# One pool of seven PSUM banks, a last attention round in two halves, and a new order of issue

## The chip, the cores and the metric

The kernel runs on one NeuronCore of a Trainium2 chip. The metric is the device time of one execution in microseconds. In the tables PE is TensorE's matmul, PEld its weight load, DVE is VectorE, ACT is ScalarE, POOL is GpSimd and SP is SyncE, which issues most of the transfers.

## What is computed

For one sequence of 2048 tokens of width 448 the kernel computes two branches of the same input and mixes them with a gate for each token:

```
g = sigmoid((x * gate_w).sum(-1))
q, k, v = split(x @ wqkv)             # 16 heads of 28
p = softmax(q @ k.T * 28**-0.5)       # per head, 2048 x 2048
a = concat_heads(p @ v) @ wo
b = irfft2(rfft2(x) * (w_r + 1j*w_i)) # over tokens and width
out = g * a + (1 - g) * b
```

The softmax has 16 x 2048 x 2048 exponentials, the largest part of the work.

## The kernel before

**Attention.** The 16 heads form four groups of four; a head takes a strip of 32 partitions. The 2048 queries are cut into four chunks of 512. A pair (group, chunk) is a round, `n` = 0 to 15 in `groups`; round 15 is the last chunk of the last group. A round runs over 16 key blocks of 128 keys, and a *unit* is one head of one key block: a score matmul of 128 keys by 512 queries (32 rows of the array, "row" layout, one of four row strips), which fills one PSUM bank of 512 float32 columns.

A unit's exponential is made in one of two ways. `ND` gives, for each round, how many key blocks go the second way.

- *ScalarE* (kind "a"): two units at a time are scored into `psA` or `psB` (two banks each, taken in turn), and one ACTIVATE (L1034) of 1024 columns writes them to the ring (`ring`, 28 slots) in bfloat16. There are 374 of these steps.
- *VectorE* (kind "d"): a unit is scored into one of three banks `bg`; a TENSOR_SCALAR (L993, "eviction") turns the score into the bits of a bfloat16 number, and GpSimd adds three constants to these bits (INT64_ADD, L1003). That gives four phases of an approximate exponential, which are averaged through the value matmuls.

The value matmuls (`pv`) are done in "column" layout, four heads side by side in four column strips of 32. Four such matmuls, one for each head, are called a quad here. A key block on ScalarE needs one quad, a key block on VectorE four, one for each phase. All quads of a round accumulate in the bank `pvb`. A column of ones in the weights gives the softmax sums.

**Normalising.** When a round is done, `normalise` copies `pvb` to SBUF (L1166), brings the sums through DRAM to the layout in which they can be inverted and multiplied (L1169, L1178), all hidden behind the next round. The last round has no round behind it: it copies all 512 queries (L1137), forms the sums by small float32 matmuls, inverts them (L1146), broadcasts them by matmuls and multiplies in two pieces of 256 (L1159). Then `last_tile` projects the last four blocks of 128 tokens (k = 0 to 3 are the spectral branch, k = 4 to 7 the four head groups; k = 7 of these waits for the normalised last round), evicts them with the gate on VectorE (L1250) or ScalarE (L1246) and stores them. The other twelve blocks of tokens go through `out_tile` (L1224).

**Background.** Projections of q, k and v, the gate and the whole spectral branch (two-dimensional transform by matmuls, `fwd`, `mid`, `inv`) run between the attention work, through the same three banks `bg`. `Item` is the right to a bank for such a piece; `bgi` gives the bank.

**Order.** Every operation is registered with `Sched.op`, and nothing is emitted until `Sched.run`. That function reads `TABLE`, two packed lists found offline: the first is the order in which all 3639 operations are emitted (with six groups of filler matmuls that write zeros into `pvb`), the second the bank of each `Item`. `pin` keeps the emitted order on every engine, and each engine's queue works strictly in that order: an operation that waits holds up all behind it on the same engine. The semaphores between engines are set by the tile framework from the tiles that instructions read and write; `psA`, `psB`, `pvb` and the three `bg` are tiles of their own. All matmuls are recorded at L432, transposes at L435.

Of the kernel before, what the change touches and what calls it, by code (L numbers as in the profile page):

```python
# [36 lines left out]
DUE_P = 4.0  # L37
TABLE = (
    "eNoN1mNjWEsUQNHxnMG5SW2ltm3bNtPUtm3btm3bto3UdvveX9hf1jakJbHEkXCCJDqJQWKSWCQ2iUPikngkPiEkAUlIEpHEJAkJI0lJMpKc"
    "UJKCZCApSU6SiniSmuQijHQlQAKiCScZSRoiSXaSlkQlitQk6Ugmkp7UILVINZKNZCG5SVUSheQhWUkOUodkJiVJKRKNlCa1SV5SloSQUFKO"  # L40
    "1Cf5SH5SgBQiBUkxUp6UIRVJYVKEFCXFySZSgWwmlUgJ0oq0JVvIVrKStCPbyHayiqwmVcgOsoZMJGtJZTKJTCZTyFSyjqwnG0g3YpVXG8l0"
    "MoPMJLOIU7PJHDKX7CTziCDzySy/gCwkcWk8Gp8uIovJDL+ELCUJaEK6jKDaRRLRnqQxWU5WkECFqMQ0Ck1Co9JoNDqNQcNoTBqLxqZx6G6y"
    "h+wl+0ioak6iqqfkGXlOXpCXJILcIQ3IfhJJ7pID5B55RV6TKOo+eUMekI7kIXlEHpNo6iCJrqaRGKouOUSS0mQ0pupEYqnkNAU9TJ6Qt2SD"
    "j63ekfckjvpA4qp4qhc5Qo6SlDS+akGOkan0I/lEptHPpAlJoBKq6fQLSaS+Qip6nCRWJ0hqmkR9gxk0TH0lp8hpkoau8WnpGXKWJFX1SG9y"
    "jpwnF8hMepEkU61JOnqJXCZXyFVyjSRX18kNcpOkULfIbZKeplRlaAaakZ4kmWhinoSnUj+hLE2t0qhYvByNzcvTXxCNz/XpVFpVgX6H6Dy9"
    "oqYiHUQyqIzqG0nGm5HvJAaPyX+Qn6Qp+UUyqT+QWf2DSjSLyqo6k+okDk/OK9OGpArtSDvRuDwhX+ezqc60C82uEvD1PhEP439IUp5D/SX/"
    "CKGUMrrac9qV5lSCSqqoprkU0Kw0G81Oc9DcKif9TXLR3NRQS/PQPCovzUdTcEfzKk/z05keaUDj83wqhBagmWlBWogWpkVofpWFhtJ4vCgt"
    "RtuTNqQ47U4LqIw8E+9BS9Ke1PJCyhhtHC+oCqv0vIjiJgMvTaUppoqqtLy4siYlr0p70RKqGi2pqtNSKh0vrVJzYXrTUlSZYaSMKkHT8Bq0"
    "Jk3FmSmrsvFyipi/UF5l5dn5SFpB5eGjaEU1mlZSeXkOPobWopVVB/IbqqiqKhcfS535AdVUTg6mNq2ucvMaqh7tQurTBjQfr0NrKm9qqc+u"
    "MC/DG9J4Bk1dWlsV4XVUDNOI1FUFeEJTkNdTCUwjmpnXV1l4WV6IJzHFeQlegefnFXkDFcs0VDFNXFOTN1KNVWNandfg8U0TVZQnMk1VMhOY"  # L50
    "YryZim1K8lo8jglXIaa5qsRb08o8mklpWqgIVY6X5m1oW9qOtlItVXnenjbjrVUqE86/uaimB2mjEpsmtK1KbkJNO1WVN6XNeQQPM9X4F9de"
    "NeFNeQeV0Xx3P9xP98t1VN1oJ1WX1+MZTDjtoprT7qSz+u0iaBTzx1XhLWhX1ZK2591UJlOKd1cduPQ9lPLpTHrTU/VSrWhtXoeDN9763iqN"
# [69 lines left out]
def unpack(table):  # L122
    raw = [zlib.decompress(base64.b64decode(t)) for t in table]
    return np.frombuffer(raw[0], np.uint16).tolist(), np.frombuffer(raw[1], np.uint8).tolist()
# [1346 lines left out]
```

## Time and profile before

| | |
|---|---|
| runs | 380.36, 381.06, 381.08 us; median 381.06 |
| profiled execution | span 379.2 us from the first to the last instruction; its own time isn't given apart, the median is 1.9 us longer |
| granted TensorE clock | 1.000 over the span |
| busy share | PE 98%, ACT 93%, DVE 89%, POOL 62% |
| exponentials on ScalarE | 374, mean 1079 ns each |
| evictions on VectorE | 276, mean 681 ns each |
| additions on GpSimd | 207, mean 1038 ns each |

A row of a timeline gives start, duration, engine, line, operation, the tile written and read, shape and count, and in brackets the idle time before it with what ended it. Matmuls are pipelined, so a duration of 0.38 us holds the way through the array, and the distance of two starts is what a matmul costs. In the same way an ACTIVATE starts before the one ahead of it has ended. A window's row gives its length and then the busy time (and number of instructions) of PE, PEld, DVE, ACT and POOL, the granted clock, the share of the DMA engines and GB/s.

### The profile page before, as it was taken

The page shows a single profiled execution, that of the slowest core. Times are in us where ns is not written, and L with a number is a line of the kernel's source. Part 1 is how long each engine was busy: PE and PEld are TensorE (multiplying, and loading weights), DVE is VectorE, ACT ScalarE, POOL GpSimd, SP SyncE. Part 2 cuts the span into 40 slices and gives each one's busy share as a digit, 9 for nine tenths or more (in the row PEclk, how much of TensorE's full clock was granted, in tenths as well). Part 3 has the DMA queues.
Part 4 walks back from the last instruction along what each step waited for, and adds up shares of the span by engine and source line. Part 5 has one row for each costly group of instructions (what it writes and reads, how often), then busy time and mean ns, then how long its engine had stood idle before and what let it go on. Part 6 is the DMA issues. An engine that isn't in the chain of part 4 may idle for free.

```text
span 379.2 us, 12643 instructions
## 1 busy us (share of the span) xinstructions
PE 371.3 (98%) x5117; PEld 142.4 (38%) x5117; DVE 339.1 (89%) x665; ACT 351.1 (93%) x389; POOL 234.4 (62%) x264
## 2 busy tenths in 40 slices
PE   8999999999999999999999999999999999999996
PEld 6634223342433333234333434233333323433564
DVE  1768899999999999999999999999999999988744
ACT  2799999999999999999999999999999999999841
POOL 4446465866778866565553565778597778483510
PEclk9999999999999999999999999999999999999999
DMA  6511101010210112211322212223222122222132
GB/s 145 157 34 44 29 18 36 4 36 2 41 52 22 44 41 54 55 38 30 68 60 93 69 40 49 57 61 70 45 64 74 30 69 72 86 64 72 35 103 75
DMA packets 31158, 21.23 MB, mean 56 GB/s; under 512 B 16260, under 2 KB 29052, under 8 KB 31100
## 3 DMA queue, kind: packets, MB, share of 16 engines
q1 hardware_dynamic: 29708, 19.96, 20.7%
q8 instruction: 40, 0.66, 0.7%
q10 hardware_dynamic: 1392, 0.46, 0.5%
q14 instruction: 18, 0.15, 0.1%
HBM read 14.51 MB, written 1.96 MB: 43 GB/s over the span
## 4 chain that ended last, share of the span: by engine, by line
PE 55%; ACT 31%; issue 6%; DVE 4%; DMA 2%; POOL 1%; SPq 0%; DVEq 0%; ACTq 0%; POOLq 0%
ACT ring L1034 31%; PE bg L432 24%; PE pvb L432 17%; PE psA L432 7%; PE psB L432 6%; DVE pd L993 2%; PE bg L435 1%; DMA CS<-cCS 1%; DVE X L1419 1%; POOL pd L1003 1%; DMA Wg<-in_B_w_i_dram 0%; DVE X L1298 0%; DVE q L1178 0%; DVE t L1362 0%; DVE wpq L1224 0%
## 5 line engine op out<-in xcount | busy, mean ns | idle before, releaser
L1003 POOL INT64_ADD pd<-pd x207 | 211.9, 1038 | 96.7 <-DVE pd L993 27.4
L1034 ACT ACTIVATE ring<-psA 128x1024 bf16<-128x1024 f32 x187 | 201.7, 1078 | 4.7 <-PE psA L432 3.2
L1034 ACT ACTIVATE ring<-psB 128x1024 bf16<-128x1024 f32 x187 | 201.7, 1079 | 2.6 <-PE psA L432 1.4
L993 DVE TENSOR_SCALAR pd<-bg 128x512 uint16<-128x512 f32 x276 | 180.9, 681 | 8.5 <-PE bg L432 3.5
L432 PE MATMUL pvb<-pd,vd 128*32 128x512 bf16 x1104 | 96.9, 384 | 0.1
L432 PE MATMUL bg<-q,k 32*128 32x512 bf16 x276 | 96.3, 383 | 0.2
L432 PEld LDWEIGHTS <-k 32*128 32x128 bf16 x1024 | 40.1, 91 | 122.4 <-issue 117.7
L432 PE MATMUL psB<-q,k 32*128 32x512 bf16 x374 | 73.2, 383 | 1.3 <-ACT ring L1034 0.7
L432 PE MATMUL psA<-q,k 32*128 32x512 bf16 x374 | 72.8, 383 | 0.5 <-ACT ring L1034 0.2
L432 PE MATMUL pvb<-ring,vw 128*32 128x512 bf16 x748 | 67.9, 384 | 0.0
L432 PEld LDWEIGHTS <-vd 128*32 128x32 bf16 x1104 | 25.3, 94 | 35.5 <-issue 31.1
L432 PEld LDWEIGHTS <-vw 128*32 128x32 bf16 x748 | 17.5, 94 | 22.7 <-issue 20.5
L432 PEld LDWEIGHTS <-xT 128*128 128x128 bf16 (+5 forms) x512 | 20.3, 97 | 10.7 <-issue 9.7
L432 PE MATMUL bg<-xT,wpq 128*32 128x512 bf16 (+3 forms) x244 | 21.2, 383 | 0.1
L1362 DVE TENSOR_TENSOR t<-bg,Wg 128x450 bf16<-128x450 f32 x32 | 18.8, 614 | 0.6 <-DMA Wg<-in_B_w_i_dram 0.4
L432 PE MATMUL bg<-xT,wpk 128*32 128x512 bf16 (+2 forms) x240 | 18.9, 383 | 0.0
L432 PE MATMUL bg<-wvr,xT 128*128 128x112 bf16 (+2 forms) x192 | 13.7, 213 | 0.0
L1178 DVE TENSOR_TENSOR q<-pvs,Rb 128x512 bf16<-128x512 f32 x15 | 10.9, 729 | 2.6 <-DMA Rb<-rsc 2.6
L1298 DVE TENSOR_TENSOR X<-bg,oc 128x226 bf16<-128x226 f32 (+1 forms) x32 | 12.3, 386 | 0.5
L432 PEld LDWEIGHTS <-CS 128*32 128x32 bf16 x384 | 9.0, 95 | 9.9 <-issue 5.6
L432 PE MATMUL bg<-xtok,CS 128*32 128x225 bf16 (+1 forms) x192 | 11.2, 294 | 0.7 <-DMA CS<-cCS 0.7
L742 DVE TENSOR_SCALAR k<-bg 128x512 bf16<-128x512 f32 x15 | 10.3, 685 | 1.3 <-PE bg L432 1.1
(117 smaller groups left out, 315.4 us busy)
## 6 DMA issues: line engine op xcount, KB each, us to landing
Rb<-rsc SPq DMA_DIRECT2D x60, 64.0 KB
CS<-cCS SPq DMA_DIRECT2D x16, 192.0 KB
V<-xtok SPq DMA_DIRECT2D x16, 113.0 KB
Wg<-in_B_w_i_dram SPq DMA_DIRECT2D x64, 28.1 KB
xtok<-Ab SPq DMA_DIRECT2D x16, 112.5 KB
xtok<-in_A_x_dram SPq DMA_DIRECT2D x3, 448.0 KB
Wg<-in_B_w_r_dram SPq DMA_DIRECT2D x32, 28.1 KB
out_dram<-wpq SPq DMA_DIRECT2D x6, 112.0 KB
```

The source lines that it names most:

```text
L432: self.pin(self.nc.tensor.matmul(out, lhsT=lhsT, rhs=rhs, start=start, stop=stop, **kw))
L435: self.pin(self.nc.tensor.transpose(out=out, in_=in_, identity=self.c("ident")[0:n, 0:n]))
L742: self.pin(nc.vector.tensor_scalar(out=dst, in0=self.bgi(it), scalar1=SQ, scalar2=None, op0=ALU.mult))
L993: self.pin(nc.vector.tensor_scalar(out=ys[:, s, :].bitcast(U16), in0=self.bgi(it), scalar1=127 * UNITS, scalar2=0.0, op0=ALU.add, op1=ALU. ...
L1003: self.pin(nc.gpsimd.int64_add(out=fl(pds), in0=fl(ys), in1=PHASE[f] * 0x0001000100010001))
L1034: self.pin(nc.scalar.activation(out=self.ring[:, u0:u0 + len(st), :], in_=slot[:, 0:len(st), :], func=ACT.Exp, scale=LN2 / UNITS))
L1178: e = self.dve(dv(512), lambda: self.pin(nc.vector.tensor_tensor(out=dst, in0=pvs[:], in1=self.Rb[:], op=ALU.mult)), ds, kk, lk=True)
L1298: self.pin(nc.vector.tensor_tensor(out=free_dims(self.X1[:, t, :], [[F, 2], [-1 if dif else 1, n]], (F - 1) * dif), in0=free_dims(self.bgi ...
L1362: self.pin(nc.vector.tensor_tensor(out=out[:], in0=self.bgi(it)[:, 0:F2].rearrange("p (a f) -> p a f", a=2), in1=free_dims(Wg[:], [[F, 2], ...
L1419: self.pin(nc.vector.tensor_tensor(out=free_dims(self.zt[0:FN], [[128, 4], [1, 128]], 512 * t), in0=self.bgi(it)[0:FN, :].rearrange("p (a ...
```

## The change

- **Banks.** `psA`, `psB` and the three `bg` become one tile `ps` of seven banks; `pvb` stays. Every score unit, the first transposes and the first projections get an `Item` and thereby any of the seven banks. A step of ScalarE reads two adjacent banks, whichever they are. An eviction on VectorE may take two adjacent banks in one instruction; `PARTS` lists how the four units of a key block can be grouped.
- **Dependencies.** Since all banks are in one tile, `pin` declares instructions that touch different banks independent, except where the operation names the other as needed (`need`) or both are on one engine.
- **Last round.** `ND` of round 15 goes from 3 to 1. Its queries are split into two halves of 256. A unit of this round covers two key blocks for one half, so that it still fills a bank (`HALF`, `tiles`, `score_mm`). Half 0 comes first, with seven ScalarE units per head and the one VectorE block; its values accumulate in a bank of the pool, those of half 1 in `pvb`. `normalise_half` normalises each half by itself.
- **Order.** `TABLE` is new and holds four lists: order (3972 operations, no fillers), banks, the number of units of each ScalarE step (378 times 2), and the grouping of the evictions of each of the 67 VectorE blocks (41 with four single ones, 24 with one pair, 2 with two pairs). A score is one operation for each unit now. `tstart` and the due times worked out from it are gone, which only served the planning.

The diff, cut to its core:

```diff
-    ND = [2,4,5,5]+[5,5,4,4]+[4,4,5,5]+[5,5,4,3]
+    ND = [2, 4, 5, 5, 5, 5, 4, 4, 4, 4, 5, 5, 5, 5, 4, 1]
...
-        self.psA = ps.tile([P, 2, 512], F32, name="psA")
-        self.psB = ps.tile([P, 2, 512], F32, name="psB")
+        self.ps = ps.tile([P, 7, 512], F32, name="ps")
         self.pv = ps.tile([P, 512], F32, name="pvb")
-        self.bgt = [ps.tile([P, 512], F32, name=f"bg{i}") for i in range(3)]
...
     def pin(self, ins):
...
+        if self.sc.used:
+            used = frozenset(self.sc.used)
+            keep = [p for p, u in self.sc.need() if not used & u]
+            if ins.ins.engine in self.before:
+                keep.append(self.before[ins.ins.engine])
+            for other in self.bank_sets:
+                if not used & other:
+                    self.tc.declare_no_dep(ins.ins, group="bank" + repr(sorted(other)), reason="other banks",
+                                           keep=[k for k in keep if k.name in self.bank_sets[other]])
...
+    HALF = [(0, i) for i in range(6)] + [(1, i) for i in range(6)] + [(1, 6), (1, 7), (0, 6), (0, 7)]
+
+    def tiles(self, n, v):
+        if n < 15:
+            return [(v, 0)]
+        kp = self.HALF[v][1]
+        return [(2 * kp, 0), (2 * kp + 1, 256)]
...
+    def score_mm(self, n, v, s, it):
+        g, c = self.groups[n]
+        w = 256 if n == 15 else 512
+        q0 = 512 * c + 256 * self.half(n, v)
+        for kt, o in self.tiles(n, v):
+            self.mm(self.bgi(it)[:, o:o + w], self.k[g][32 * s:32 * s + 32, 128 * kt:128 * kt + 128],
+                    self.q[g][32 * s:32 * s + 32, q0:q0 + w], True, True, tile_position=(32 * s, 0))
...
+                    self.pin(nc.vector.tensor_scalar(
+                        out=free_dims(ys[:], [[512 * e, w], [1, 512]], 512 * part[0]).bitcast(U16),
+                        in0=self.ps[:, bs[0]:bs[0] + w, :],
+                        scalar1=127 * UNITS, scalar2=0.0, op0=ALU.add, op1=ALU.max))
...
+                self.pin(nc.scalar.activation(out=self.ring[:, u0:u0 + len(st), :],
+                                              in_=self.ps[:, bs[0]:bs[0] + len(st), :],
+                                              func=ACT.Exp, scale=LN2 / UNITS))
...
+    def normalise_half(self, h, last, it):
...
+        o = 256 * h
+        ev = self.dve(0.42, lambda: self.pin(nc.vector.tensor_copy(out=pvs[:, o:o + 256], in_=bank()[:, 0:256])),
+                      last + [self.nlast[1]], -100.0)
...
+        def fsum():
+            for j in range(2):
+                self.mm(bank()[:, 256 + 4 * j:260 + 4 * j], pvs[:, o + P * j:o + P * j + P], rows, True, True)
+        m = self.pe(1024, fsum, [ev, self.d_cst2], kk, dur=0.45)
+        b = self.dve(0.2, lambda: self.pin(nc.vector.reciprocal(out=rr[:, 8 * h:8 * h + 8], in_=bank()[:, 256:264])),
+                     (m, self.nlast[1]), kk)
...
+        mb = self.pe(1024, fb, [b, self.d_idf], kk, mode="col", dur=0.45)
+        e = self.dve(0.42, lambda: self.pin(nc.vector.tensor_tensor(out=dst, in0=pvs[:, o:o + 256], in1=bank()[:, 0:256],
+                                                                    op=ALU.mult)), (mb,), kk, free=it)
+        self.onormt[12 + 2 * h] = self.onormt[13 + 2 * h] = e
```

455 lines of the change are left out of this document (243 added, 212 removed).

## The prediction

> **What bounds the kernel now.** I read the page first, then ScalarE's own rows in order of time, the busy time by windows, the groups kept apart by shape, and last the timeline of TensorE around one switch of work and around the end.
>
> ```profile
> PE 371.3 (98%) x5117; PEld 142.4 (38%) x5117; DVE 339.1 (89%) x665; ACT 351.1 (93%) x389; POOL 234.4 (62%) x264
> PE 55%; ACT 31%; issue 6%; DVE 4%; DMA 2%; POOL 1%; SPq 0%; DVEq 0%; ACTq 0%; POOLq 0%
> ```
>
> Three engines are nearly full, and the chain that ended last runs mostly through PE, a third through ScalarE. The rows of ScalarE say which of them gives the pace, and where.
>
> ```profile
> L1034 ACT ACTIVATE ring<-psA 128x1024 bf16<-128x1024 f32 x187 | 201.7, 1078 | 4.7 <-PE psA L432 3.2 <-PE psB L432 1.3 <-ACT ring L1034 0.2
> L1034 ACT ACTIVATE ring<-psB 128x1024 bf16<-128x1024 f32 x187 | 201.7, 1079 | 2.6 <-PE psA L432 1.4 <-PE psB L432 1.2
> ...
> 12.74 1.02 ACT L1034 ACTIVATE ring<-psA 128x1024 bf16<-128x1024 f32 x1 [0.31 <-PE psB L432]
> ...
> 17.32 1.02 ACT L1034 ACTIVATE ring<-psA 128x1024 bf16<-128x1024 f32 x1
> ...
> 20.03 1.06 ACT L1034 ACTIVATE ring<-psB 128x1024 bf16<-128x1024 f32 x1
> ...
> 156.00 1.02 ACT L1034 ACTIVATE ring<-psA 128x1024 bf16<-128x1024 f32 x1 [0.16 <-ACT ring L1034]
> ...
> 199.61 1.02 ACT L1034 ACTIVATE ring<-psA 128x1024 bf16<-128x1024 f32 x1 [0.46 <-PE psB L432]
> ...
> 341.94 1.05 ACT L1034 ACTIVATE ring<-psA 128x1024 bf16<-128x1024 f32 x1
> ...
> 364.96 1.02 ACT L1034 ACTIVATE ring<-psB 128x1024 bf16<-128x1024 f32 x1
> ```
>
> One exponential lasts 1.02, but the next starts before it ends: from 17.32 to 20.03 three steps take 2.71, so 0.903 us a step when nothing is missing. There are 374, hence 373 steps, 336.8 us. From the first at 12.74 to the last at 364.96 pass 352.2, so ScalarE loses 15.4 us between them. The rows numbered 154, 198 and 352 say where: 44 steps from 156.00 to 199.61 (39.7 due, 43.6 taken) lose 3.9, 21 steps from 341.94 to the end lose 4.1, and the other 308 steps lose 7.4. The windows agree:
>
> ```profile
> 160.00:200.00 40.00, 40.00 (x584) 14.99 (x588) 38.95 (x77) 37.52 (x42) 22.09 (x23) 1.00 0.20 48
> 200.00:340.00 140.00, 137.74 (x1789) 49.07 (x1785) 135.65 (x277) 139.69 (x153) 97.76 (x99) 1.00 0.25 62
> 340.00:366.00 26.00, 26.00 (x482) 11.89 (x486) 17.39 (x28) 22.84 (x25) 10.63 (x11) 1.00 0.26 75
> 366.00:379.20 13.20, 9.67 (x244) 7.02 (x236) 6.80 (x12) 1.55 (x2) 0.00 (x0) 0.99 0.22 72
> 40.00:340.00 300.00, 296.91 (x3993) 104.15 (x3996) 290.09 (x577) 297.01 (x325) 204.07 (x208) 1.00 0.19 48
> ```
>
> Where ScalarE (fourth busy figure) falls back, 37.52 of 40 and 22.84 of 26, PE is busy without a gap. So the time is: 12.7 until the first exponential, 336.8 of steps, 15.4 lost in them, and 14.2 from the start of the last one to 379.2. The median of the runs, 381.06, lies 1.9 us above this span; I add that to every span below.
>
> **What the edits cost, by part.** *More exponentials.* The last round gives two key blocks, eight units of 512 columns, back to ScalarE. Its 378 steps of two units (the list of widths in the new table holds 378 twos) are four more: +3.6 us at 0.903. Nothing hides them.
>
> *TensorE.* Prices first.
>
> ```profile
> 346.12 0.39 PE L432 MATMUL psB<-q,k 32*128 32x512 bf16 x2
> 346.44 0.39 PE L432 MATMUL bg<-wpk,q 128*32 128x448 bf16 x4
> ...
> 347.30 0.40 PE L432 MATMUL pvb<-ring,vw 128*32 128x512 bf16 x4
> 347.52 0.39 PE L432 MATMUL pvb<-pd,vd 128*32 128x512 bf16 x4
> 347.85 0.39 PE L432 MATMUL bg<-q,k 32*128 32x512 bf16 x1
> 347.85 0.39 PE L432 MATMUL psB<-q,k 32*128 32x512 bf16 x2
> 347.86 0.38 PE L432 MATMUL bg<-q,k 32*128 32x512 bf16 x1
> 348.17 0.40 PE L432 MATMUL pvb<-ring,vw 128*32 128x512 bf16 x4
> ```
>
> Four value matmuls side by side follow the next four after 0.22 (347.30 to 347.52). From values to scores it is 0.33 (347.52 to 347.85), from scores to the next group 0.32: each change between the row layout of the scores and the column layout costs 0.10 more. And two scores (346.12) or four in four strips (347.85) cost the same 0.32. So a run of scores costs 0.2 for entering and leaving and 0.217 for each set of different strips. Unpacked, the old order has 357 such runs with 381 sets, the new one 317 with 360: 40 x 0.2 + 21 x 0.217 = 12.6 us less. A key block on VectorE takes four phases of values, one on ScalarE a single one: two blocks moved save 2 x 3 quads, 1.3 us. Six filler groups go, 0.6. By these prices the whole order falls from 351.7 to 337.2 us. In the last round each score becomes two matmuls of 256 columns; whether the second set of weights is hidden no row shows in the row layout, so 0 (as for 224 columns in column layout below) to 64 x 0.09 / 3 = 1.9 us; I take 0.
>
> ```profile
> 353.33 0.56 PE L432 MATMUL bg<-Bd,X 113*32 113x224 bf16 x16
> ...
> L432 PEld LDWEIGHTS <-k 32*128 32x128 bf16 x1024 | 40.1, 91 | 122.4 <-issue 117.7
> ```
>
> Four such quads take 0.56, the last itself 0.27: 0.10 a quad, no weights seen.
>
> *VectorE and GpSimd.*
>
> ```profile
> 347.67 2.48 DVE L993 TENSOR_SCALAR pd<-bg 128x512 uint16<-128x512 f32 x4
> ...
> L993 DVE TENSOR_SCALAR pd<-bg 128x512 uint16<-128x512 f32 x276 | 180.9, 681 | 8.5 <-PE bg L432 3.5 <-PE psB L432 1.2 <-PE psA L432 0.9
> L1315 DVE CAST Ab<-bg 128x450 bf16<-128x450 f32 x16 | 9.8, 618 | 0.1
> ```
>
> Four evictions in 2.48, the last 0.68 long, are 0.60 apart. A column costs (681 - 618) / 62 = 1.02 ns, so 512 columns 0.52 and an instruction 0.08 (bounds 0 and 0.16, the fixed part of the 681). The parts list merges 28 pairs and eight evictions are gone, 240 instead of 276: 8 x 0.60 + 28 x 0.08 = 7 us less. GpSimd loses six additions; it is 62% busy. Neither shortens the chain by itself.
>
> *What this does to the lost 15.4.* I cut both orders into stretches of 22 exponentials (19.9 us of ScalarE) and price the work listed in each. After the start, PE stands clearly above 19.9 in three of the old: 154 to 198 with 21.4 and 21.7 (3.3 over; 3.9 were lost) and 352 to 374 with 22.2. That is where the rows lose time, so I trust the count. After, 154 to 198 comes to 39.0, below; new heavy ones are 198 to 220 (PE 21.4, VectorE 21.7), VectorE at 132 (20.9) and 308 (20.5), and the end (PE 21.4). Lost after: 154 to 198 0.7; 198 to 220 1.8 + 0.3; 132 1.0 + 0.2; 308 0.6 + 0.3; the end 4.1 - 0.8 = 3.3. The other steps lost 5.1 before. In the old order a step is mostly listed with only its own two units scored (312 of 374); with seven common banks the new one has four or six ready at 210 of 378, so a late score is covered by 0.9 us or more. I take 3.0 (bounds 1.7 and 5.1). Sum 11.2, a gain of 4.2.
>
> *The end.*
>
> ```profile
> 366.55 0.69 DVE L1137 COPY pvs<-pvb 128x512 f32<-128x512 f32 x1 [0.17 <-PE pvb L432]
> 367.80 1.05 PE L432 MATMUL pvb<-cst,pvs 128*128 128x4 f32 x8
> 368.89 0.26 DVE L1146 RECIPROCAL rr<-pvb 128x16 f32<-128x16 f32 x1 [0.40 <-PE pvb L432]
> ...
> 369.46 0.61 PE L432 MATMUL pvb<-sq,rr 128*32 128x128 f32 x16
> 370.15 0.42 DVE L1159 TENSOR_TENSOR q<-pvs,pvb 128x256 bf16<-128x256 f32 x1 [1.00 <-PE pvb L432]
> ...
> 371.40 0.62 PE L432 MATMUL pvb<-sq,rr 128*32 128x128 f32 x16
> 372.33 0.40 DVE L1159 TENSOR_TENSOR q<-pvs,pvb 128x256 bf16<-128x256 f32 x1
> ...
> 375.28 0.39 PE L432 MATMUL bg<-wpk,q 128*32 128x448 bf16 x4
> ```
>
> Call E the start of the last exponential. Before, its values are copied from E + 1.6, the second half is normalised at E + 7.8, the last projection starts at E + 10.3, and 3.9 us later all is over (eviction, store). After, half 0 is normalised among the exponentials of half 1 (its copy, sums and products are work for engines counted above). From the last four scores, some 1.4 before E, the order lists 3.7 us of projections and other values before the last value quad: it starts at E + 2.6. Copy of 256 columns (0.42, as 370.15) to E + 3.4; five projections, then the two sums at E + 3.6, 0.55 (half of 1.09); reciprocal to E + 4.4; broadcast 0.3 + 0.7; product to E + 5.8, beside which PE works off 13 projections, to E + 7.0; the two that needed it, the last starting at E + 7.2; 3.9 behind: E + 11.1. Gain 3.1; bounds 1.5 (PE late by its stretch) and 5 (the 3.7 us done earlier).
>
> Sum: 12.7 + 377 x 0.903 (340.4) + 11.2 + 11.1 = 375.4, and 1.9: **377.3 us**. DMA issues stay as many; their new places on SP's queue I price at nothing, since SP waits in hidden time except where the rows lose it.
>
> **The rivals.** *The lead hides more.* If the earlier scores absorb all but the two heaviest PE stretches (1.8 and 3.3), 5.1 is lost instead of 11.2: 371.2. For it: the idle time on the rows of the exponentials (4.7 and 2.6) ends almost all with a score, and PE has 14 us less to do. Against: VectorE stays as full.
>
> *PE was not what held ScalarE, or its saving is not real.* Then 15.4 stays lost: 12.7 + 340.4 + 15.4 + 11.1 + 1.9 = 381.5, no change. For it: scores come one unit per operation now, 756 operations instead of 374, each of which may signal. Against: 347.85 (three operations) takes no longer than 346.12 (one). The Trainium skill (TensorE: Matmul & The Clock Gate, The cost: per-tile semaphore tail) states 26.3 ns for each signalling tile, one after the other; 382 of them would be an estimated 10 us and eat most of PE's gain, giving about 380. By that rule this rival; the trace shows no such tail for three.
>
> *Slower: VectorE stops ScalarE.* Before, the banks of ScalarE's scores were freed by ScalarE alone. Now any bank may wait for VectorE, and a pair is freed together; behind a waiting score the whole PE queue stands. Place: every score run whose bank VectorE held last. Price: VectorE's idle time from 40 to 340, 300 - 290.1 = 9.9 us (it waits there for scores and for transfers), each a stall passed on: up to 387.2; at two thirds, 384. It decides when more than 4.5 of the 9.9 reach ScalarE. Against: four or six units lie ready.
>
> **How the numbers follow.** Forecast 0.52, more lead 0.22, no gain 0.12, VectorE 0.14. The forecast's own range, with excess 8 to 14 and end 9.5 to 12.5, is 373 to 380. A difference under 0.2%, 0.8 us, can't be told from none. Faster (below 380.3): 0.51 + 0.22 + 0.02 = 0.75; within: 0.08; slower: 0.14 + 0.03 = 0.17. The range for 8 in 10 reaches to the lead's 371 and to the no-gain case: 370.5 to 382.
>
> **What would show it.** 378 steps at 0.903; the start of the last exponential near 364; less than 1 us lost between steps 154 and 198 and about 2 between 198 and 220; 240 evictions, pairs near 1.2 us; 11 us after the last exponential's start. Wrong would be: gaps on ScalarE released by VectorE's banks, runs of four scores above 0.33, or PE without a gap at unchanged length.

## The result: 387.5 us, 1.3% slower, and the profile after

The changed kernel took 385.63, 384.20, 389.45 and 391.24 us, median 387.54, against a median of 381.07 for the kernel before on the same chip (380.36 to 381.61), 1.7% more by the medians. The ratio is 1.0135, 95% interval 1.0097 to 1.0173; here and below a ratio leaves out any execution more than 1.5% above the shortest of its kernel, here the longest. The forecast was 377.3. The mean granted clock of the four was 0.996, 1.000, 0.981 and 0.982, so it differs from execution to execution. In the kernel before, measured again beside the runs below, it was 0.998 or more in all executions but one, and 0.996 in that one. The profiled one has a span of 383.9 and its own time 385.63, so 1.7 lie around the span.

First the page: busy time by engine, and the chain that ended last.

```profile
span 383.9 us, 12664 instructions
PE 368.9 (96%) x5209; PEld 149.7 (39%) x5209; DVE 334.3 (87%) x631; ACT 354.9 (92%) x393; POOL 227.9 (59%) x258
PE 59%; ACT 17%; DVE 11%; DMA 5%; issue 4%; SPq 2%; POOL 1%; ACTq 0%; DVEq 0%; POOLq 0%
```

VectorE and GpSimd have less to do, as forecast. The chain has left ScalarE (31% before, 17% now) for TensorE (55 to 59), VectorE (4 to 11) and transfers (2 to 5). Next the groups, shapes kept apart, and ScalarE's waits, after the change and then before it.

```profile
L1051 DVE TENSOR_SCALAR pd<-ps 128x512 uint16<-128x512 f32 x212 | 138.6, 683 | 4.7 <-PE ps L464 3.6 <-POOL pd L1065 0.2
L1051 DVE TENSOR_SCALAR pd<-ps 128x1024 uint16<-128x1024 f32 x28 | 34.2, 1221 | 1.3 <-PE ps L464 0.8
L1100 ACT ACTIVATE ring<-ps 128x1024 bf16<-128x1024 f32 x378 | 349.7, 1107 | 10.5 <-PE ps L464 10.3
ACT ring L1100 <- PE ps L464: 10.3, 17, 1.5
```

```profile
ACT ring L1034 <- PE psA L432: 4.5, 8, 0.8
ACT ring L1034 <- PE psB L432: 2.5, 6, 0.6
```

240 evictions, a pair at 1.22 us, 378 exponentials: the counts are as forecast. A line of waits gives the sum in us, how many there were and the longest: ScalarE waited 10.3 us for scores in only 17 places, and 7.0 us in 14 places before. The same windows as before the change:

```profile
160.00:200.00 40.00, 39.73 (x575) 15.00 (x577) 38.80 (x75) 37.89 (x42) 24.63 (x27) 1.00 0.20 50
200.00:340.00 140.00, 134.02 (x1733) 49.99 (x1725) 132.91 (x255) 138.40 (x152) 92.63 (x94) 1.00 0.25 62
340.00:372.00 32.00, 31.72 (x702) 17.81 (x706) 19.97 (x31) 28.37 (x31) 10.66 (x10) 1.00 0.26 79
```

TensorE now has 6 us of idle time between 200 and 340 (2.3 before), and ScalarE gets nothing for it: 138.40 of 140, 139.69 before. Last, ScalarE's timeline at its start and its end.

```profile
11.92 1.94 ACT L1100 ACTIVATE ring<-ps 128x1024 bf16<-128x1024 f32 x2 [0.16 <-PE ps L464]
15.36 1.02 ACT L1100 ACTIVATE ring<-ps 128x1024 bf16<-128x1024 f32 x1 [1.50 <-PE ps L464]
...
371.49 1.94 ACT L1100 ACTIVATE ring<-ps 128x1024 bf16<-128x1024 f32 x2 [1.32 <-PE ps L464]
```

The first exponential starts at 11.92 (12.74 before), the last at 371.49 + 0.92 = 372.41, and all ends 11.4 us later (14.2 before). Between them lie 377 steps of 0.903, 340.4 us, in 360.5: ScalarE loses 20.1 us (15.4 before, 11.2 forecast). The span's growth of 4.7 is 3.6 (four steps) + 4.7 (lost) - 2.8 (end) - 0.8 (start).

Where it is lost, in us between the exponentials named, from the starts of all exponentials in four profiles (the last two kernels are explained below):

| exponentials | before | forecast | after | after, again | with zero groups | and multiply moved |
|---|---|---|---|---|---|---|
| 0 to 22 | 1.4 | | 4.9 | 2.2 | 2.1 | 3.0 |
| 22 to 154 | 2.8 | over 1.2 | 2.6 | 2.6 | 2.6 | 2.6 |
| 154 to 198 | 3.9 | 0.7 | 3.6 | 3.9 | 3.8 | 3.5 |
| 198 to 286 | 1.5 | over 2.1 | 1.4 | 1.4 | 1.6 | 1.9 |
| 286 to 330 | 1.3 | over 0.9 | 2.4 | 2.6 | 3.2 | 2.4 |
| 330 to the last | 4.6 | over 3.3 | 5.1 | 5.3 | 4.8 | 4.5 |
| sum | 15.4 | 11.2 | 20.1 | 18.1 | 18.2 | 17.9 |

The stretch that was to be relieved, 154 to 198, is as it was. What the change lost beyond the kernel before lies elsewhere: at the start, from 286 to 330 and at the end.

### The profile page after: what moved, and what is told of

It reads as the page before. It is cut to its first block, busy times and chain, and to the rows that moved or that the text cites. A ratio compares the mean times of both kernels' runs of the same rounds, so it can differ in the third digit from the quotient of the medians.

```text
span 383.9 us, 12664 instructions
## 1 busy us (share of the span) xinstructions
PE 368.9 (96%) x5209; PEld 149.7 (39%) x5209; DVE 334.3 (87%) x631; ACT 354.9 (92%) x393; POOL 227.9 (59%) x258
## 4 chain that ended last, share of the span: by engine, by line
PE 59%; ACT 17%; DVE 11%; DMA 5%; issue 4%; SPq 2%; POOL 1%; ACTq 0%; DVEq 0%; POOLq 0%
PE ps L464 40%; PE pvb L464 18%; ACT ring L1100 16%; DVE pd L1051 5%; SPq L439 2%; DMA xtok<-in_A_x_dram 2%; DVE t L1439 1%; PE ps L467 1%; DMA X<-in_A_wqkv_dram 1%; DMA out_dram<-wpk 1%; DMA wpq<-in_A_wo_dram 1%; DMA Rb<-rsc 1%; POOL pd L1065 1%; DVE X L1496 1%; DVE q L1220 0%
## 5 line engine op out<-in xcount | busy, mean ns | idle before, releaser
L1100 ACT ACTIVATE ring<-ps 128x1024 bf16<-128x1024 f32 x378 | 349.7, 1107 | 10.5 <-PE ps L464 10.3
L1051 DVE TENSOR_SCALAR pd<-ps 128x512 uint16<-128x512 f32 (+1 forms) x240 | 171.4, 746 | 6.0 <-PE ps L464 4.4
L464 PE MATMUL ps<-q,k 32*128 32x512 bf16 (+1 forms) x1088 | 144.2, 370 | 4.8 <-ACT ring L1100 1.0
L464 PE MATMUL pvb<-ring,vw 128*32 128x512 bf16 (+1 forms) x760 | 65.2, 375 | 0.3 <-DVE pvs L1208 0.3
L464 PE MATMUL ps<-xT,wpq 128*32 128x512 bf16 (+3 forms) x248 | 19.4, 382 | 0.4 <-DVE wpq L578 0.2
L1439 DVE TENSOR_TENSOR t<-ps,Wg 128x450 bf16<-128x450 f32 x32 | 18.8, 618 | 0.6 <-issue 0.3
L464 PE MATMUL ps<-xT,wpk 128*32 128x512 bf16 (+3 forms) x244 | 18.9, 398 | 0.0
L464 PEld LDWEIGHTS <-CS 128*32 128x32 bf16 x384 | 9.9, 95 | 10.2 <-issue 5.0
L792 DVE TENSOR_SCALAR k<-ps 128x512 bf16<-128x512 f32 x15 | 10.3, 688 | 3.2 <-PE ps L464 3.1
L464 PE MATMUL ps<-wvr,xT 128*128 128x112 bf16 x192 | 12.9, 213 | 0.1
L1375 DVE TENSOR_TENSOR X<-ps,oc 128x226 bf16<-128x226 f32 (+1 forms) x32 | 12.3, 387 | 0.6
L464 PE MATMUL ps<-wpq,q 128*32 128x448 bf16 x128 | 11.8, 364 | 0.0
L792 DVE TENSOR_SCALAR q<-ps 128x512 bf16<-128x512 f32 x15 | 10.3, 687 | 1.5 <-PE ps L464 1.3
```

The costliest lines, as they stand in the source:

```text
L464: self.pin(self.nc.tensor.matmul(out, lhsT=lhsT, rhs=rhs, start=start, stop=stop, **kw))
L792: self.pin(nc.vector.tensor_scalar(out=dst, in0=self.bgi(it), scalar1=SQ, scalar2=None, op0=ALU.mult))
L1051: self.pin(nc.vector.tensor_scalar(out=free_dims(ys[:], [[512 * e, w], [1, 512]], 512 * part[0]).bitcast(U16), in0=self.ps[:, bs[0]:bs[0] ...
L1100: self.pin(nc.scalar.activation(out=self.ring[:, u0:u0 + len(st), :], in_=self.ps[:, bs[0]:bs[0] + len(st), :], func=ACT.Exp, scale=LN2 / ...
L1375: self.pin(nc.vector.tensor_tensor(out=free_dims(self.X1[:, t, :], [[F, 2], [-1 if dif else 1, n]], (F - 1) * dif), in0=free_dims(self.bgi ...
L1439: self.pin(nc.vector.tensor_tensor(out=out[:], in0=self.bgi(it)[:, 0:F2].rearrange("p (a f) -> p a f", a=2), in1=free_dims(Wg[:], [[F, 2], ...
```

## The experiments

**Parts of the change.** Four kernels on one chip, with 380.87 us before. One is the changed kernel unaltered.

> The changed kernel once more, unaltered, to see how its time spreads and whether a longer execution goes with a lower granted TensorE clock. Theory A (a stall of TensorE in the first 20 us lets the clock fall): times between 384 and 391 us, the longer ones with the lower mean clock, the loss of ScalarE's steps again near 4 to 5 us in the first 22 steps and near 15 in the others. Theory B (the spread is spread over the whole kernel): the loss in the first 22 steps is as before the change, 1.4 us.

Measured: 387.60 us (384.09 to 388.66), ratio 1.0161 (1.0109 to 1.0213); clock 0.998, 0.982, 1.000 and 0.987. The result stands. One execution took 386.76 us at clock 1.000, so the clock is not the whole spread. In this profile the start had no stall for a transfer, and lost 2.2 instead of 4.9.

In the changed kernel's own profile TensorE's rows at the start, and windows of them, were these:

```profile
13.48 0.60 PE L467 MATMUL ps<-cst,xtok 128*97 128x128 bf16 x7 [1.43 <-DMA xtok<-in_A_x_dram]
```

```profile
14.00:16.00 2.00, 2.00 (x29) 1.18 (x30) 1.39 (x3) 0.64 (x1) 0.05 (x1) 0.80 0.57 143
16.00:18.00 2.00, 2.00 (x19) 0.51 (x12) 0.17 (x1) 1.07 (x2) 2.00 (x4) 0.50 0.08 22
18.00:20.00 2.00, 2.00 (x20) 1.12 (x19) 1.80 (x4) 1.81 (x3) 0.96 (x2) 0.84 0.00 0
```

Transposes of the last quarter of x stand ahead of the next scores and wait 1.43 us; then the granted clock (the figure behind the five busy times) is 0.50. The second kernel moves these transposes back.

```diff
 TensorE's order at the start
-8 x transpose of x, block 3; 16 x value projection; scores of exponentials 2 and 3
+16 x value projection; scores of exponentials 2 and 3; 8 x transpose of x, block 3
```

> One move in the order: the eight transposes of token block 3 (they wait for a transfer) go behind the 16 value projections of block 0 and the first two scores of key block 1. Theory A (that wait, with the clock it costs, is the loss at the start): the first 22 steps lose 1 to 2 us instead of 4.9, span 3 to 3.5 us shorter than the changed kernel's 383.9, near 380.5, median near 382 and all runs at clock 1.000. Theory B (another queue or the new banks slow the start): the same span within 1 us.

Measured: 390.06 us (388.28 to 390.40), ratio 1.0231 (1.0199 to 1.0262). The start lost 3.5 us, not clearly less, and the clock was halved somewhere else:

```profile
298.00:301.00 3.00, 1.40 (x18) 0.52 (x18) 3.00 (x6) 1.97 (x3) 2.95 (x3) 1.00 0.09 17
301.00:304.00 3.00, 3.00 (x29) 0.64 (x25) 2.55 (x6) 2.47 (x3) 1.39 (x2) 0.54 0.21 37
304.00:307.00 3.00, 3.00 (x26) 0.51 (x22) 1.26 (x4) 2.19 (x3) 2.69 (x3) 0.50 0.23 48
```

In the first of these windows TensorE was busy for 1.40 of 3.00 us; then the clock stood at 0.50 from 301.3 on for 13.7 us. In 384 us that makes a mean of 0.982, the figure of the long executions. So the clock became a suspect that no rival of the forecast had.

The third is the kernel before, with all banks in one tile and the declared independences, its order unchanged; the fourth the changed kernel with every pair of evictions made as two.

```diff
-        self.psA = ps.tile([P, 2, 512], F32, name="psA")
-        self.psB = ps.tile([P, 2, 512], F32, name="psB")
+        self.ps = ps.tile([P, 7, 512], F32, name="ps")
...
+                    self.tc.declare_no_dep(ins.ins, group="bank" + repr(sorted(other)), reason="other banks",
```

> The kernel before with its order and bank use unchanged, but with the two score tiles and the three background tiles laid into one tile of seven banks, and with the declarations of independence that the change brings. Theory A (the order is what costs, the tile is neutral): 381 us within 0.3%. Theory C (one tile for all banks adds waits): slower by 2 us or more, with idle time on ScalarE released by VectorE or TensorE where there was none.

```diff
 the changed kernel, the grouping of evictions
-24 key blocks with one pair, 2 with two pairs
+all 67 key blocks with four single ones
```

> The changed kernel with each paired eviction split into two single ones at the same place (268 instead of 240). Theory D (a pair holds two banks too long and TensorE's queue stands behind it): 1 to 4 us faster than the changed kernel. Theory A (VectorE is not what limits): within 0.5 us, or up to 2 us slower in the stretches where VectorE is full, since 28 instructions of 0.06 to 0.08 us come back.

Measured: 380.83 us, ratio 1.0003 (0.9991 to 1.0015), and 385.69 (384.40 to 389.33), ratio 1.0142 (1.0089 to 1.0196). One tile costs nothing, pairs bring nothing that can be seen. What is left is the order with its banks, and the last round.

**The clock, and whose work counts.** With 380.97 us before. The first kernel adds 25 groups of four matmuls on zeros into `pvb`, about 2.7 us of TensorE, in rounds 9 to 14, ahead of operations for which TensorE waited there. The others build on it: 12 value quads of round 7 or of round 10 left out, or four exponentials narrowed.

```diff
+groups of zero columns, filler(-2, 256), 25 times in rounds 9 to 14
```

> The changed kernel with 25 filler groups (zeros, 256 columns, 0.107 us each) put ahead of scores, value quads and transforms in rounds 9 to 14 that TensorE was seen to wait for, as the kernel before has six. Theory E (the saved work leaves TensorE idle there long enough that its clock is halved): no time at half clock behind 200 us, all executions within 1% of each other, near 384 us, median 3 us lower than the changed kernel's 387.5. Rival (the spread has another origin): the same spread from 384 to 391 us, or all executions 2 to 3 us longer by the added work.

```diff
 def fm(...):
+    if kind == "d" and f[0] and n == 7:
+        return
```

> The kernel with fillers, leaving out 12 of the 16 value quads of VectorE's key blocks in round 7 (phases 1 to 3; 12 x 0.217 = 2.6 us of TensorE work), so that round 7's values are wrong. Round 7 is where ScalarE lost 3.7 us. Theory A (ScalarE sets the pace, TensorE only in the stretches where its work exceeds 19.9 us for 22 steps): 2 to 2.6 us shorter than with fillers alone, the loss of steps 154 to 198 near 1.5. Rival F (VectorE or the banks it holds set the pace there): less than 1 us shorter.

```diff
 def fm(...):
+    if kind == "d" and f[0] and n == 10 and kt != 12:
+        return
```

> The kernel with fillers, leaving out 12 value quads (2.6 us of TensorE work) in round 10 instead, whose values are then wrong. Theory A: no change within 0.5 us, since ScalarE's steps follow at 0.903 there and TensorE waits already. Rival G (TensorE's total sets the time everywhere): 2.6 us shorter as in round 7.

```diff
-in_=self.ps[:, bs[0]:bs[0] + len(st), :],
+w = 16 if i in (238, 242, 246, 250) else 512
+in_=self.ps[:, bs[0]:bs[0] + len(st), 0:w],
```

> The kernel with fillers, in which four exponential steps of round 10 do only 16 of their 512 columns per unit (the rest of these units isn't computed). Each then takes some 0.2 instead of 0.903 us. Theory A: 2.5 to 3 us shorter. Rival G (TensorE's total sets the time): within 0.5 us. This is the price, with sign reversed, of the four steps that the change adds.

Measured. With the zero groups: 384.66 us (383.20 to 384.69), ratio 1.0089 (1.0061 to 1.0117), all four executions at clock 1.000. More work on TensorE made the kernel 3 us shorter at the median. I take that for the clock's share, and the best of the executions without the groups (384.1 and 384.2) lie where these do. The size is rough: the two intervals of the ratio overlap a little.

Without the quads of round 10: 389.31 us (387.89 to 391.21), all at clock 0.977 to 0.982, that is 4.6 us longer for 2.6 us less of work. TensorE's waits and the windows say how:

```profile
PE ps L462 <- ACT ring L1098: 0.9, 3, 0.4
```

```profile
254.00:257.40 3.40, 2.75 (x25) 0.90 (x22) 3.31 (x8) 3.40 (x5) 2.64 (x4) 1.00 0.12 22
257.40:261.00 3.60, 3.60 (x37) 0.99 (x33) 2.41 (x6) 2.83 (x4) 3.24 (x4) 0.50 0.22 42
261.00:267.00 6.00, 5.79 (x42) 1.14 (x40) 4.99 (x7) 5.12 (x6) 3.36 (x4) 0.50 0.30 74
267.00:271.10 4.10, 4.10 (x45) 1.24 (x43) 2.50 (x7) 3.20 (x4) 2.97 (x3) 0.51 0.01 4
271.10:275.00 3.90, 3.83 (x52) 1.19 (x52) 3.77 (x9) 3.77 (x5) 1.13 (x2) 1.00 0.60 154
```

TensorE was busy 2.75 of 3.40 us, with waits of at most 0.4 for ScalarE's banks, and was then granted half its clock for 13.7. The Trainium skill (TensorE: Matmul & The Clock Gate, A second HAM failure mode: psum-queue depth-cycling) describes a kernel in which short idle times between groups of matmuls, as PSUM banks go round, let the clock fall and rise. The rows agree in kind: apart from 1.00 they show 0.50, and 0.51 in a window that ends a little behind the change. This fall is the odd one, though: in the five other profiles in which the clock fell later than at 30 us, TensorE had been busy for 1.4 to 2.2 of the 3.41 us ahead, and windows with 2.0 to 2.5 passed elsewhere without a fall. No run shows a busy share that decides.

Without the quads of round 7: 386.12 us (384.84 to 387.33), ratio 1.0130 (1.0090 to 1.0170). The stretch 154 to 198 still loses 3.9 us, though it has fewer quads to do; after it, the clock was halved for 3.4 us near 310. The narrowed exponentials: 386.11 (383.72 to 389.53), ratio 1.0115; four steps with 3.3 us less of ScalarE shorten their stretch, 220 to 264, by 0.4 us, since the exponentials behind them wait (1.66 and 1.26 us from start to start). So neither TensorE's amount of work in the one stretch nor ScalarE's in the other is what counts alone.

**VectorE, the fillers of before, and one wait.** With 381.30 us before.

```diff
-in0=self.ps[:, bs[0]:bs[0] + w, :],
+cw = 16 if n in (7, 10) else 512
+in0=self.ps[:, bs[0]:bs[0] + w, 0:cw],
```

> The kernel with the 25 groups of zero columns (384.66 us), in which the VectorE evictions of rounds 7 and 10 read and write 16 of the 512 columns of each bank (31 banks, about 0.6 us of VectorE each; the powers of these key blocks are left out for the other columns). They lie between exponentials 166 and 189 and between 243 and 260. Without the change ScalarE loses 1.37 + 2.40 us between exponentials 154 and 198, where taking 2.6 us of value products from TensorE did not shorten anything. Theory VectorE (it runs 97% there and sets when banks come free): the loss between 154 and 198 falls from 3.8 us to 1.5 or less, the one between 220 and 264 (0.65) below 0.4. Theory order of TensorE (scores are placed too late whatever VectorE does): 3 us or more stay between 154 and 198. The whole time would be 382 to 383 us by the first and 384.5 by the second, if the clock stays at 1.00; VectorE idle may let TensorE wait less, so that the clock is not the risk it was where its work was cut.

```diff
 the same, and for ScalarE
+w = 16 if i in (166, 170, 174, 178, 238, 242, 246, 250) else 512
```

> The kernel before this one (short evictions in rounds 7 and 10), and exponentials 166, 170, 174, 178, 238, 242, 246 and 250 of 16 of 512 columns each as well: 8 x 0.8 = 6.6 us of ScalarE work left out. With full evictions four of them (238 to 250) shortened their stretch by 1 us of 3.3. Theory VectorE held it: now the stretches 154 to 198 and 220 to 264 are each at least 2 us shorter than with the short evictions alone. Theory TensorE held it (97% busy there): they are shorter by less than 1 us each, and the waits of ScalarE for scores grow by the rest.

```diff
 the kernel before, its order
-six groups of filler matmuls
```

> The kernel before, without its six filler groups of zero columns (0.6 us of TensorE work that computes nothing); all else as it was. Theory clock (these fillers keep the granted clock up where TensorE waits): some executions show the clock at half for 3.4 or 13.7 us, and the median is 1.5 to 6 us above 380.97. Theory that the fillers do nothing: 380.5 to 381.3, clock 1.00.

```diff
 VectorE's order in round 10, with the zero groups
-eviction pair, multiply by Rb, 4 x product t, eviction pair
+eviction pair, 4 x product t, multiply by Rb, eviction pair
```

> The kernel with the 25 groups of zero columns (384.66 us), in which VectorE's multiply that normalises round 10 (it waits 1.94 us for the transfer of Rb at 294.9 us, with four products of the gate's round behind it) stands behind these four products in VectorE's order. Theory: the stall of VectorE there is what ScalarE loses between exponentials 286 and 330 (1.82 + 1.41 us), so 1.0 to 1.9 us come back: 382.8 to 383.7. Rival: the transfer is late for the step behind it in any case, or the next wait takes its place: 384.3 to 385. With fewer waits the half clock should be no likelier than before.

Measured. Short evictions: 384.47 us (383.80 to 388.24), ratio 1.0121 (1.0057 to 1.0184); these are the windows from 155 to 200, first with full and then with short evictions, each from its own kernel.

```profile
155.00:200.00 45.00, 44.56 (x641) 16.60 (x641) 43.60 (x85) 42.73 (x47) 25.46 (x27) 1.00 0.19 47
```

```profile
155.00:200.00 45.00, 44.82 (x645) 16.34 (x641) 36.74 (x85) 42.93 (x48) 25.42 (x27) 1.00 0.20 47
```

VectorE went from 43.60 to 36.74 of 45, and the loss from 154 to 198 from 3.8 to 3.6. My theory of VectorE fell. With the eight exponentials narrowed as well (384.01 us, ratio 1.0081, 1.0051 to 1.0111) the stretches 154 to 198 and 220 to 264 are 0.3 and 0.9 us shorter, of 3.3 each: by its expectation, TensorE. (Its profile is of the longest execution, whose clock was low from 14 to 24 us only, ahead of both.)

The kernel before without its fillers: 381.05 us, ratio 0.9993 (0.9981 to 1.0005), clock 0.998 or more. So the six fillers of before kept nothing up, and my account that their loss had lowered the clock fell too. What differs is how much TensorE idles. These are two windows near 300, first in the kernel before, then in the changed one.

```profile
296.00:300.00 4.00, 3.87 (x56) 1.30 (x50) 4.00 (x11) 4.00 (x6) 3.38 (x4) 1.00 0.16 26
300.00:304.00 4.00, 3.93 (x59) 1.41 (x55) 3.90 (x9) 4.00 (x6) 3.54 (x4) 1.00 0.36 83
```

```profile
296.00:300.00 4.00, 3.67 (x60) 1.54 (x59) 2.58 (x5) 4.00 (x5) 1.88 (x3) 1.00 0.20 48
300.00:304.00 4.00, 3.09 (x44) 1.05 (x41) 4.00 (x9) 3.17 (x5) 2.36 (x3) 1.00 0.20 33
```

The multiply moved: 383.07 us (382.43 to 383.40), ratio 1.0050 (1.0033 to 1.0066), 1.6 us less. VectorE's timeline with the zero groups alone, and then with the move:

```profile
293.07 1.82 DVE L1049 TENSOR_SCALAR pd<-ps 128x1024 uint16<-128x1024 f32 x2
296.83 0.69 DVE L1218 TENSOR_TENSOR q<-pvs,Rb 128x512 bf16<-128x512 f32 x1 [1.94 <-DMA Rb<-rsc]
297.44 2.22 DVE L1437 TENSOR_TENSOR t<-ps,Wg 128x450 bf16<-128x450 f32 x4
```

```profile
295.82 1.16 DVE L1437 TENSOR_TENSOR t<-ps,Wg 128x450 bf16<-128x450 f32 x2 [1.31 <-PE ps L462]
297.29 1.16 DVE L1437 TENSOR_TENSOR t<-ps,Wg 128x450 bf16<-128x450 f32 x2 [0.31 <-ACT ring L1098]
298.37 1.38 DVE L1218 TENSOR_TENSOR q<-pvs,Rb 128x512 bf16<-128x512 f32 x1
```

The products no longer stand behind the wait for the transfer. In the profiles 0.8 of the 1.6 us lies between exponentials 286 and 330 (the loss at 315, 1.24, is gone, and 302 now loses 0.80); 0.5 lies ahead of exponential 22, long before the move. So the move is shown to be worth 0.8, and the rest is open. This is the fastest form of the changed order found here, still slower than before.

**Is it the place of the scores?** With 380.84 us before. In the trace of this last kernel I compared, for each late exponential, when its score started with when the banks it writes had come free, and moved scores up to that point: sixteen, or only the four between exponentials 150 and 210. (Below, vmm is a matmul of a value projection and wtr a transpose for the weights of the values.)

```diff
 TensorE's order, e.g. at exponentials 196 and 201
-7 x projection, scores 196
+6 x projection, scores 196, projection
-5 x vmm, wtr, 3 x vmm, wtr ..., scores 201
+scores 201, 5 x vmm, wtr, 3 x vmm, wtr ...
```

> The kernel with the multiply moved and the 25 groups of zero columns (383.07 us), with the score products of 16 late exponentials moved up in TensorE's order, each to where the banks that it writes had come free in the trace (0.2 to 1.5 us earlier: past one or two projections, evictions' scores, value quads, output products). Nothing is left out, no work is less. Theory order (ScalarE waits because a score stands behind other TensorE work though its banks are free): of the 9 us lost at these 16 exponentials the smaller of loss and room, about 5 us, is the most that can come back; half of it is given back at the next score, so 380 to 381.5 us. Rival: the work that the scores are moved past is then late for VectorE and GpSimd, and the time stays at 382.5 to 384.

> The same with only the four moves between exponentials 150 and 210 (185, 191, 196, 201). The stretch 154 to 198, where 2.6 us less of TensorE work and 9 us less of VectorE work changed nothing, loses 3.5 us. Theory order: these moves give back 0.8 to 1.4 us in 154 to 220, and the rest stays where the banks themselves come free late (exponentials 161 and 170, whose scores start within 0.2 us of their banks): 381.7 to 382.3. Rival: the loss comes back at the next scores; 383.

Measured: 387.13 us (386.62 to 387.76), ratio 1.0161 (1.0139 to 1.0183), and 384.54 (384.11 to 385.03), ratio 1.0095 (1.0071 to 1.0120). Both slower than 383.07. With the four moves the loss at exponential 185 is gone and that at 196 went from 1.04 to 0.77, but exponentials 198 and 201 now lose 0.52 and 0.68: from 154 to 220 it is 4.9 us in place of 4.1. That is what the rival expected.

**Two engines' work together, and one place.** With 381.09 us before (381.81 for the last).

```diff
 short evictions and no quads of round 7; then the eight exponentials too
+cw = 16 if n in (7, 10) else 512
+if kind == "d" and f[0] and n == 7: return
```

> The kernel with the 25 groups of zero columns and both cuts at once: the 12 value quads of round 7 left out (9 of them, about 2 us of TensorE, are issued between exponentials 176 and 198, where by themselves they left a loss of 2.48 us) and the evictions of rounds 7 and 10 of 16 columns (by themselves 2.19 us). Theory that TensorE and VectorE bound the stretch together, each closing the gap that the other leaves: the loss between 176 and 198 falls to 0.3 to 1.2 us. Theory that it is the order of scores, projections and banks as written: it stays at 1.8 us or more.

> The same with the eight exponentials of 16 columns as well (166, 170, 174, 178, 238, 242, 246, 250). Theory that TensorE, VectorE and ScalarE are each full in this stretch: 154 to 198 is 2 to 3 us shorter than with the two cuts, of the 3.3 that the four exponentials save. Theory order as written: less than 1 us shorter, as the scores do not come earlier.

```diff
-self.mm4(self.bgi(it), self.wpad[w, g][0:n, c, :], self.xT[b][0:n, c, :], c == 0, stop and c == 3)
+self.mm4(self.bgi(it)[:, 0:z], self.wpad[w, g][0:n, c, :], self.xT[b][0:n, c, 0:z], c == 0, ...)
+    z = 64 if (w, g, b) == ("k", 3, 0) else 512
```

> The kernel with the 25 groups of zero columns, in which the last four of the seven projections that stand in TensorE's order between the score pair of exponential 195 and that of 196 (28 matmuls in 1.71 us) work on 64 of 512 columns (k of one block of 512 tokens is left out for the others): 0.7 to 0.8 us of TensorE less, at this one place. Theory order as written (a score pair can be issued ahead of its exponential by no more than its banks allow, so what stands between two pairs counts there and nowhere else): the loss at exponential 196, which stayed 0.98 to 1.11 us with 2 us of value products and 9 us of evictions away, falls to 0.4 us or less, and 154 to 198 from 3.8 to 3.2 or less. Rival, that the exponential waits for something else at this place: it stays at 0.9 or more.

Measured. Both cuts: 386.28 us (385.22 to 388.31), ratio 1.0122 (1.0094 to 1.0151); 176 to 198 loses 1.9 us, the loss at exponential 196 being 1.1. With the exponentials too: 384.15, ratio 1.0080 (1.0055 to 1.0105); 154 to 198 loses 3.1 in place of 3.3, though it has 3.3 us less of ScalarE, 2 of TensorE and 7 of VectorE to do. The sum of no engine's work explains this; what is left is the order as written. Four of the seven projections before exponential 196 narrowed: five executions took 383.68 to 385.33 us, median 384.40, ratio 1.0077 (1.0043 to 1.0110); a sixth took 1041.02 us, which nothing here explains. First TensorE's timeline before this edit, with the zero groups alone, then with it:

```profile
195.87 0.39 PE L462 MATMUL ps<-q,k 32*128 32x512 bf16 x2
196.18 1.71 PE L462 MATMUL ps<-xT,wpk 128*32 128x512 bf16 x28
197.82 0.39 PE L462 MATMUL ps<-q,k 32*128 32x512 bf16 x4
```

```profile
195.73 0.96 PE L462 MATMUL ps<-xT,wpk 128*32 128x512 bf16 x28
197.03 0.40 PE L462 MATMUL ps<-q,k 32*128 32x512 bf16 x4 [0.35 <-ACT ring L1099]
```

The projections are 0.75 us shorter, but the next score gains only a part: it now waits 0.35 for banks that exponential 195 holds. ScalarE's rows at exponential 196, before and with the edit:

```profile
198.31 1.02 ACT L1098 ACTIVATE ring<-ps 128x1024 bf16<-128x1024 f32 x1 [0.86 <-PE ps L462]
```

```profile
197.52 1.02 ACT L1099 ACTIVATE ring<-ps 128x1024 bf16<-128x1024 f32 x1 [0.54 <-PE ps L462]
```

The loss there fell from 0.98 to 0.67, between the two theories, and the stretch 154 to 198 from 3.8 to 3.2. So 0.3 were the projections, and a wait for banks is what remains at 196. These 0.75 us less between two score pairs shortened the stretch by 0.5; the 2 us less of TensorE or 7 less of VectorE, each by itself, had changed it by 0.2 at most.

**The banks.** That row led to a count in the order lists: which exponential frees the banks that a score pair writes. With the multiply moved, of 377 pairs 278 write what the exponential two steps before their own frees (0.04 us lost each), and six what the exponential *just* before frees. These six (6, 170, 196, 366, 369, 371) lose 0.91 each, 5.5 us of 17.9: exponential, score and exponential follow one another. In the kernel before `psA` and `psB` take turns, so this cannot happen there. The last kernel trades banks at four of the six.

```diff
 banks and TensorE's order at exponentials 170, 196, 366, 371
-8 x out; scores 366 in banks 6, 5; scores 367 in banks 1, 0
+6 x out; scores 366 in banks 1, 0; 2 x out; scores 367 in banks 6, 5
```

> The kernel with the multiply moved and the 25 groups of zero columns (383.07 us). In its order lists 6 of the 377 score pairs write banks that the exponential just before their own frees (exponentials 6, 170, 196, 366, 369, 371), and at these six ScalarE loses 5.5 of its 17.9 us; the 278 pairs whose banks are freed by the exponential before that lose 0.04 each. Here four of them (170, 196, 366, 371) trade banks with the pair behind them, whose banks were already free, and are moved up past one to four projections or output products. Theory banks: the loss at these four falls from 0.82 + 1.04 + 0.83 + 0.85 to 1.0 or less together, the stretches 154 to 198 and 352 to 378 each lose 1 us less, and the time is 381 to 382 us. Rival, TensorE is full there anyway (busy 44.6 of 45 us and 25 of 25), so that its work behind the moved scores is late by as much: what is won at these four is lost at the next two or three scores, 383 us.

Measured: 385.56 us (384.75 to 389.80), ratio 1.0153 (1.0093 to 1.0213), against 380.96. The losses at 196, 366 and 371 fell to 0.12, 0.38 and 0.30, that at 170 stayed (0.78), and 172, 198, 368 and 373 now lose 0.66, 0.85, 0.71 and 1.39; 154 to 198 went from 3.5 to 4.6, 352 to the last from 4.1 to 4.9.

At first this looks like the rival again. But by the new order lists the trade itself made two new places of the kind: 198 and 368 now write what the exponential just before frees, which they did not before the trade. And 170 was given a bank that a small ACTIVATE frees just ahead of its exponential. These are TensorE's row for the two scores of 170, of which the second starts at 171.78, and ScalarE's rows:

```profile
171.39 0.76 PE L462 MATMUL ps<-q,k 32*128 32x512 bf16 x2
```

```profile
171.41 0.32 ACT L861 ACTIVATE w<-ps 128x64 f32<-128x64 bf16 x1
172.19 1.94 ACT L1098 ACTIVATE ring<-ps 128x1024 bf16<-128x1024 f32 x2 [0.46 <-PE ps L462]
```

So at three of its four places the trade moved the cause on and did not remove it, and the bank theory was not refuted. For 172 and 373 nothing of the kind is in the lists; there the rival fits, that TensorE's work between two scores is late.

## Why the prediction was wrong

- **Pace, steps, end: right.** 378 steps of 0.903, +3.6 us with nothing to hide them. The end is E + 11.4 (forecast 11.1; before 14.2). Its steps nearly held: the last value matmuls started at E + 2.7 (forecast 2.6) and the reciprocal ended at E + 4.6 (4.4); the product ended at E + 6.9 instead of 5.8.
- **TensorE 14.5 us less: right in the main, and worth nothing.** An estimate from the starts of all matmuls in the two profiles, each kind priced by its usual distance from the next, gives 10 to 14 us less of work; the waits of more than 0.12 us on top of these prices grew by 11 to 14. The tail for each signalling tile that the Trainium skill states (TensorE: Matmul & The Clock Gate, The cost: per-tile semaphore tail), which would have eaten the gain, does not show: three scores take 0.32 us up to the next group whether one, two or three of them signal (carry a semaphore update), and 649 score matmuls signal where 607 did, not 382 more. The saving was waited away. The rival that held it for unreal (381.5) came nearer than the forecast, for another reason.
- **VectorE and GpSimd: nearly right in size** (VectorE 339.1 to 334.3 busy, 4.8 less where 7 were forecast; 240 evictions), and off the path, as 7 us less between 155 and 200 showed.
- **Lost steps 15.4 to 11.2: the step that failed.** It was 20.1 and 18.1 in two profiles. Two terms of the sum failed. The stretch 154 to 198, put at 0.7, lost 3.6 and 3.9. The other steps, put at 3.0 because scores would lie ready, lost 9.4 and 7.0 (5.1 before): the larger miss. The stretch 198 to 220, put at 2.1, lost 0.55, so the count missed both ways. I summed the listed work over 22 exponentials and took a stretch to lose what exceeds 19.9 us. That counts only if a score can be made well ahead, so that a light step pays for a heavy one. The line "four or six ready at 210 of 378" was read off the order of issue and left out the banks: with seven of them, 278 of 377 pairs write banks that the exponential two before frees. In the traces the last score of a pair starts 0.58 us ahead of its exponential at the median, as it did before the change. The lead that was to cover the other steps did not exist for most pairs, so a gap between two scores counts mostly by itself. From 154 to 198 the loss remained, as far as the runs show, because of the projections between two score pairs at 196 and two pairs on the banks of the exponential just before; the cuts of 2 to 7 us, all three together, left 3.1. What made the start and 286 to 330 worse than before the change is not shown, but for the late transfer and the multiply.
- **The slower rival (VectorE stops ScalarE) had the sign and, with 384 to 387.2, the nearest time, but not the mechanism.** One of its stalls was real, the multiply that waits for `Rb` (0.8 us shown). The rest was not: in rounds 7 and 10 VectorE's evictions could be cut without effect.
- **What no rival had: the clock.** About 3 us of the median. With less to do, but no fewer places to wait, TensorE idled in pieces, and five of the eight executions of the unaltered changed kernel had a mean clock of 0.981 to 0.996.

The balance at full clock, with the zero groups: +3.6 (steps) - 2.8 (end) + 2.8 (lost, 18.2 against 15.4) + 0.1 (start) = +3.7, measured 384.66 - 380.97 = 3.7. With about 3 for the clock it is the 6.5 of the result.

What stays open: no order was run that is free of pairs on the banks of the exponential just before, so it isn't shown what such an order would gain, nor that a full TensorE gave the loss back in the last kernels. These six pairs make 5.5 of the 17.9 us; the kernel before has none and loses 15.4. Nor is it shown what decides whether the clock falls for 3.4 or for 13.7 us. No order was found that beats the kernel before.

## What to carry to other kernels

Work taken from a full engine is worth something only where the order lets the next engine use it: count from one hand-over to the next, with the buffers that the hand-over needs and who frees them, and sum over a stretch only as far as the buffers let work run ahead. In a hand-written order look for producers that write a buffer which the consumer's step just before frees; each such place cost 0.6 to 1.3 us here, and after a trade of banks count again, since it can make new ones. And when TensorE's work is cut and its waits stay, look at the granted clock of every execution before believing a time.

## What the runs showed of the hardware

The granted clock halved although TensorE was busy 2.75 of the 3.40 us ahead, with no wait over 0.4, and stayed at 0.50 for 13.7 us in two kernels and for 3.4, 6.8 or 10.2 in others. Taking 2.6 us of work away made a kernel 4.6 us slower, adding 2.7 us of matmuls on zeros made one 3 us faster. The Trainium skill (TensorE: Matmul & The Clock Gate, What's actually happening) ties the low clock to at least one idle window of about 3.4 us; the lengths here agree with that unit (13.7 is four of 3.4), the idle window does not: TensorE was four fifths busy in the one ahead of this fall, and 1.4 to 2.2 us of 3.41 ahead of five others.
